# A Strassen-type matmul chain on one core: the last quad of the first up stage in another product order, its block sums a tick sooner, down slabs converted as soon as their area is open

## The chip, the cores and the metric

One Trainium2 chip, one of its cores. The metric is the device time of one execution in microseconds (us); a kernel's time is the median of three runs. Engines are named as in the profile: PE is TensorE's matmul, PEld its weight load, DVE is VectorE, ACT ScalarE, POOL GpSimd, SP SyncE, whose queue issues the DMAs.

## The reference

Attention over 4 batches, 12 heads, 448 tokens of width 64, then two dense feed-forward blocks on the 1792 x 768 result:

```
q_n, k_n = rmsnorm(q, g_q), rmsnorm(k, g_k)
attn = softmax(q_n @ k_n.T / sqrt(64)) @ v          # 4 x 12 x 448 x 64
x = attn as 1792 x 768
h = maximum(x @ w_in, 0.0);  x = (h * h) @ w_out    # first block, hidden width 2048
g = x @ w_gate                                       # second block, hidden width 1536
out = (silu(g) * (x @ w_val)) @ w_out2
```

The weights arrive in double precision, q, k and v in single; the result is wanted in single.

## The kernel before

The attention comes first and is not touched. The two blocks follow, each as an up stage and a down stage: up stage 0 (`w_in`), down stage 0 (`w_out`), up stage 1 (`w_gate`, `w_val`), down stage 1 (`w_out2`). Activations lie transposed, features on the 128 partitions and tokens along the row, 448 tokens to a slot of the tile `xacc`.

Every matrix product is done by seven products P1 to P7 on 2 x 2 blocks instead of eight (a Strassen form with the block sums T1 to T4). Each operand is split in a high part, rounded to the matmul's format, and a low part, the rest, so that a product of two 128-blocks is three matmuls: high x high, high x low, low x high. ACT makes a high part by a cast, DVE the low part by a subtraction. Weights' parts lie in a ring of five buffers (`ring`), activations' parts in units (`xab`, `xat`, `xb`, `xlast`).

*Up stage.* The loop `up` runs over quads (pairs of weight slabs, 8 in stage 0, 12 in stage 1), products and two token halves `tp`. One step is 9 matmuls of 128 x 448. A step's result is taken out of PSUM by ACT or DVE (`after`, `outer`), passed through relu and square by ACT (`finish_sum`), and becomes a block B11, B12, B21 or B22 of the hidden activations. DVE forms the sums T1 to T4 of these (`sum_of`), at the due times that `put` sets. Each block that the down stage needs is sent to DRAM (`send`, L1056, name `hid`).

*Down stage.* The loop `down` runs over 7 products x 8 groups g (6 in stage 1) in the order P2 P5 P3 P1 P6 P7 P4. One step is 18 matmuls. For step n a load brings the hidden block back (`stage`, L1269, `dn<-hid`) into one of three staging places, ACT casts its high part (`cleave(n, 0)`, L1282), DVE subtracts the low part (`cleave(n, 1)`, shown with the helper's line L1097); the parts go in one of three `hbuf` buffers. The load of step n + 3 needs the staging place that the low part of step n empties. Down weights lie in the area `dn`: half of the slabs of stage 0 were converted early and kept in DRAM, and are fetched again (`bring`, L380, `dn<-wkeep`); six slabs are converted straight into the area (`area_job`): double precision arrives as two 32-bit words, ACT writes the scaled high word (L292), DVE does one TENSOR_SCALAR (L294) and two SCALAR_TENSOR_TENSOR (L265). In the second block all slabs are kept ones, so there is no area job.

*What sets the order.* The program's order is written by Python at build time. Each engine works its instructions off in this order. After every step `pump` gives DVE a budget in us (1.2 a step in the up stage; unspent budget is carried over, up to 2.0), and takes from two streams, weights for the ring and conversions, what it pays for. Block sums (`run_sums`) and the cleaves follow behind. The list `where` says which unit holds which activation part, `hsplit` which units the `hbuf` buffers take over, and `open_down` puts the area in the place of the units 7 to 12 (`xb`) once the last product that reads them is done. In the last quad the order is P1, P4 of the quad before, P5, P6, P2, P7, P3, and P4 closes the stage; the area opens behind P7.

The gate of `area_job` before the change asks that a down step has begun:

```
yield act(lambda: None, gate=lambda: state["step"] >= 100 * ph)
```

## Time and profile before

| | |
|---|---|
| three runs | 1133.16, 1138.66, 1143.78 us, median 1138.66 |
| the profiled execution | 1143.64 us, its span 1141.8 us |
| PE busy | 1124.7 us, 99% of the span |
| DVE busy | 872.8 us, 76% |
| ACT busy | 637.0 us, 56% |
| granted TensorE clock | 1.000 |

The span runs from the first to the last instruction; the execution's own time is 1.84 us longer. Up stage 0 ends at 458.39 us and up stage 1 at 982.08 us in the span. A matmul's end in the profile is modelled, so lengths of matmul groups overlap; starts are the better measure.

### The profile page before, as it was taken

How to read it: one execution, taken by the hardware profiler on the slowest of the kernel's cores; microseconds unless marked ns; L12 is line 12 of the kernel's file. 1: busy time of each engine (PE TensorE's matmuls, PEld its weight loads, DVE VectorE, ACT ScalarE, POOL GpSimd, SP SyncE). 2: the span in 40 equal slices, each digit the busy share in tenths (PEclk: the TensorE clock that was granted, in tenths of full speed). 3: DMA queues.
4: the chain of work that ended last, by engine and by line, in shares of the span. 5: the costliest groups of instructions: out<-in, count | busy, mean ns of one | idle time of the engine just before them, and what ended most of it. 6: DMA issues, size and time to landing. Idle time of an engine off the chain costs nothing.

```text
span 1141.8 us, 17075 instructions
## 1 busy us (share of the span) xinstructions
PE 1124.7 (99%) x6164; PEld 946.3 (83%) x6164; DVE 872.8 (76%) x1253; ACT 637.0 (56%) x1047; POOL 212.2 (19%) x220
## 2 busy tenths in 40 slices
PE   8999999999999999999999999999999999999998
PEld 5555555559899999899999999999999999989998
DVE  7677888759998886998557778978787795775554
ACT  6787887656866776545544545444443434355332
POOL 5899899841000000000000000000000000000000
PEclk9999999999999999999999999999999999999999
DMA  5444322111888988966443302646464651784553
GB/s 169 122 114 126 102 92 83 47 30 30 256 297 257 305 279 269 366 211 204 157 122 121 113 1 100 227 157 208 135 210 132 211 185 53 241 287 136 179 169 138
DMA packets 116676, 189.60 MB, mean 166 GB/s; under 512 B 13936, under 2 KB 97648, under 8 KB 116592
## 3 DMA queue, kind: packets, MB, share of 16 engines
q1 hardware_dynamic: 116272, 188.52, 51.4%
q8 instruction: 48, 0.79, 0.3%
q14 instruction: 36, 0.29, 0.1%
q10 hardware_dynamic: 320, 0.00, 0.0%
HBM read 129.11 MB, written 59.20 MB: 165 GB/s over the span
## 4 chain that ended last, share of the span: by engine, by line
PE 87%; DVE 5%; DMA 3%; ACT 2%; issue 2%; SPq 1%; POOL 0%; DVEq 0%; POOLq 0%; ACTq 0%
PE ps L1135 40%; PE ps L1324 29%; PE s L789 6%; PE s L774 6%; PE s L745 2%; PE s L713 2%; PE s L810 2%; DVE xacc L1097 1%; PE s L754 1%; ACT xacc L1100 1%; DVE xacc L127 1%; DVE ring L268 1%; DMA raw<-in_k_dram 1%; DMA raw<-in_q_dram 1%; DVE xb L150 1%
## 5 line engine op out<-in xcount | busy, mean ns | idle before, releaser
L1135 PE MATMUL ps<-xb,ring 128*128 128x448 f32 x1080 | 228.7, 367 | 0.3 <-ACT xacc L1100 0.3
L1135 PEld LDWEIGHTS ps<-xb,ring 128*128 128x128 f32 x1080 | 202.7, 188 | 19.9 <-ACT xacc L1100 0.7
L1324 PE MATMUL ps<-xat,ring 128*128 128x448 f32 x1008 | 208.7, 368 | 2.7 <-DVE xat L1097 2.7
L1324 PEld LDWEIGHTS ps<-xat,ring 128*128 128x128 f32 x1008 | 189.1, 188 | 22.1 <-DVE xat L1097 3.4
L1135 PE MATMUL ps<-xat,ring 128*128 128x448 f32 x720 | 157.5, 367 | 0.0
L1324 PE MATMUL ps<-xab,ring 128*128 128x448 f32 x756 | 154.5, 366 | 1.8 <-ACT xacc L1348 1.6
L1324 PEld LDWEIGHTS ps<-xab,ring 128*128 128x128 f32 x756 | 141.6, 188 | 14.5 <-ACT xacc L1348 2.4
L1135 PEld LDWEIGHTS ps<-xat,ring 128*128 128x128 f32 x720 | 135.2, 188 | 12.8
L1100 ACT ACTIVATE xacc<-ps 128x448 f32<-128x448 f32 x148 | 79.3, 543 | 104.0 <-PE ps L1135 92.7
L1097 DVE TENSOR_TENSOR xacc<-ps,xacc 128x448 f32<-128x448 f32 x164 | 100.1, 619 | 37.5 <-PE ps L1135 23.4
L265 DVE SCALAR_TENSOR_TENSOR conv<-xacc,conv 128x768 int32<-128x768 int32 x124 | 119.7, 965 | 3.6
L1100 ACT ACTIVATE xacc<-xacc 128x448 f32<-128x448 f32 x148 | 85.0, 577 | 66.8 <-DVE xacc L1097 64.3
L1135 PE MATMUL ps<-xab,ring 128*128 128x448 f32 x540 | 117.7, 367 | 0.0
L748 DVE TENSOR_REDUCE mxz<-s 112x2 f32<-112x896 f32 x96 | 100.4, 1089 | 19.2 <-PE s L745 19.0
L1135 PEld LDWEIGHTS ps<-xab,ring 128*128 128x128 f32 x540 | 101.3, 188 | 10.3 <-issue 0.7
L1282 ACT CAST xat<-dn 128x896 fp32r<-128x896 f32 x56 | 52.9, 944 | 100.6 <-PE ps L1324 64.1
L268 DVE TENSOR_TENSOR ring<-conv,ring 128x384 fp32r<-128x384 f32 x127 | 70.7, 566 | 43.3 <-ACT ring L513 42.1
L780 POOL TENSOR_TENSOR sg<-p 112x896 f32<-112x896 f32 x46 | 96.8, 2106 | 15.0 <-ACT p L776 15.0
L776 ACT ACTIVATE p<-s 112x896 f32<-112x896 f32 x96 | 87.9, 920 | 20.7 <-PE s L774 16.3
L1097 DVE TENSOR_TENSOR xat<-dn,xat 128x896 fp32r<-128x896 f32 x56 | 60.9, 1088 | 37.8 <-ACT xat L1282 37.7
L1097 DVE TENSOR_TENSOR xacc<-xacc 128x448 f32<-128x448 f32 x148 | 88.1, 618 | 1.2
L1282 ACT CAST xab<-dn 128x896 fp32r<-128x896 f32 x42 | 39.6, 944 | 77.8 <-PE ps L1324 60.4
(97 smaller groups left out, 1361.8 us busy)
## 6 DMA issues: line engine op xcount, KB each, us to landing
hid<-xacc SPq DMA_DIRECT2D x196, 224.0 KB
dn<-hid SPq DMA_DIRECT2D x98, 448.0 KB
xacc<-in_moe_w_out_dram SPq DMA_DIRECT2D x28, 768.0 KB
xacc<-in_moe_w_in_dram SPq DMA_DIRECT2D x16, 768.0 KB
xacc<-in_moe_w_gate_dram SPq DMA_DIRECT2D x12, 768.0 KB
xacc<-in_moe_w_val_dram SPq DMA_DIRECT2D x12, 768.0 KB
wkeep<-conv SPq DMA_DIRECT2D x22, 384.0 KB
dn<-wkeep SPq DMA_DIRECT2D x44, 192.0 KB
```

Of the source, the lines that this page charges most:

```text
L265: nc.vector.scalar_tensor_tensor(out=out, in0=in0, scalar=scalar, in1=out, op0=op, op1=ALU.bitwise_or)
L268: nc.vector.tensor_tensor(out=out, in0=a, in1=b, op=ALU.subtract)
L748: nc.vector.tensor_reduce(out=mxz[:, c, 0:P:D], in_=ps[:CP, :, :S], op=ALU.max, axis=AX.X)
L774: nc.tensor.matmul(ps[:CP, a, :S], lhs, rhs, start=(w == 0), stop=(w == 3))
L776: nc.scalar.activation(out=p, in_=ps[:CP, :, :S], func=AF.Exp)
L780: nc.gpsimd.tensor_tensor(out=sg, in0=p_t[pi, 2 * w], in1=p_t[pi, 2 * w + 1], op=ALU.add)
L789: nc.tensor.matmul(ps[s, :S], v_t[pi][:, a, c * D:(c + 1) * D], p[:, a, :], start=(c == 0), stop=(c == NCH - 1),)
L1097: eng.tensor_tensor(out=o, in0=a, in1=b, op=op)
L1100: nc.scalar.activation(out=slot(s), in_=src, func=func)
L1135: nc.tensor.matmul(ps, w[:, wi, kk * P:(kk + 1) * P], xk[:, xi, kk * S:(kk + 1) * S], start=bool(first and mm == 0), stop=(mm == 3 * KT - ...
L1282: nc.scalar.copy(k[:, 0], src)
L1324: nc.tensor.matmul(ps_of(ps[tp, o]), w[:, wi, o * P:(o + 1) * P], h[:, hi, tp * S:(tp + 1) * S], start=bool(first and m == 0), stop=(g == ...
```

## The change

1. In up stage 0 the last quad runs P1, P5, P6, P3, P2, P7, P4 (P4 of the quad before still behind P1) instead of P1, P5, P6, P2, P7, P3, P4. The weight of P3 is formed in the scratch buffer `s_`, so that P2's weight block is left whole. The area opens behind P2, which is again four steps ahead of the stage's end; the loads, fetches and first cleaves that hung on P7 and P3 hang on P2 and P7 (`final`). Up stage 1 keeps its order.
2. Two activation parts change places (`where`), and the `hbuf` buffers lie in `xab` in down stage 0 and in `xat` in down stage 1 (`hsplit`), the other way round than before.
3. For the last group the sum T3 is due after 1 tick instead of 2 and T2 after 2 instead of 3, in both up stages; T1 after 1 instead of 2 in stage 0.
4. An area job may start as soon as the area is open, instead of at the first down step.

```
-        (dict(zip(names, (0, 1, 2, 3, 12, 4, 6))), dict(zip(names, (7, 8, 5, 9, 10, 11, 13)))),
-        (dict(zip(names, (0, 7, 6, 2, 8, 9, 3))), dict(zip(names, (1, 10, 13, 5, 11, 12, 4)))),
+        (dict(zip(names, (0, 1, 2, 3, 12, 4, 6))), dict(zip(names, (7, 8, 11, 9, 10, 5, 13)))),
+        (dict(zip(names, (0, 7, 6, 4, 8, 9, 1))), dict(zip(names, (3, 10, 13, 5, 11, 12, 2)))),
...
-    hsplit = (3, 0)
+    hsplit = (1, 3)
+    final = (("P2", "P7"), ("P7", "P3"))
...
-                mid.extend((p, q_) for p in ("P5", "P6", "P2", "P7", "P3"))
+                mid.extend((p, q_) for p in (
+                    ("P5", "P6", "P3", "P2", "P7") if (ph, q_) == (0, n - 1) else ("P5", "P6", "P2", "P7", "P3")))
...
     def area_job(ph, f, i):
-        yield act(lambda: None, gate=lambda: state["step"] >= 100 * ph)
+        yield act(lambda: None, gate=lambda: dn.get("ph") == ph)
...
+                    if (ph, q_) == (0, nq - 1):
+                        yield dve(0.55, minus, s_, a12, a11, gate=idle_("s"))
+                        yield from block((ph, "P3", q_), s_, "s")
+                        yield from block((ph, "P2", q_), a12, key(q_, "a12"), since=lambda: -1, done=over(q_, 0))
+                        yield from block((ph, "P7", q_), a21, key(q_, "a21"), since=lambda: -1)
+                        continue
...
-            for new, needs, wait in (("T1", ("B11", "B12"), 1 + end), ("T3", ("B22", "T1"), 2),
-                                     ("T2", ("B22", "T1"), 3), ("T4", ("B21", "T2"), 2 - end)):
+            for new, needs, wait in (("T1", ("B11", "B12"), 1 + end * ph), ("T3", ("B22", "T1"), 2 - end),
+                                     ("T2", ("B22", "T1"), 3 - end), ("T4", ("B21", "T2"), 2 - end)):
...
-            if last and (p, tp) in (("P3", 1), ("P4", 0)):
-                early = ("P3", "P4").index(p)
+            if last and (p, tp) in ((final[ph][1], 1), ("P4", 0)):
+                early = int(p == "P4")
...
-                if q_ == last and tp == 1 and p == "P7":
+                if q_ == last and tp == 1 and p == final[ph][0]:
                     open_down(ph)
...
-                if q_ == last and p == "P3":
+                if q_ == last and p == final[ph][1]:
                     bring(ph, 1 + 2 * tp)
```

Line numbers in the changed kernel are 1 to 8 higher: L1105 there is L1097 here, L1064 L1056, L1275 L1269, L266 L265, L295 L294, L269 L268, L252 L251, L382 L380.

Three places show what the change moves.

DVE at the end of up stage 0, in the kernel before, from the last result taken out of PSUM (`xacc<-ps_3373`) on. `ring1_83` is the low part of the first down weight, `xat<-dn` a low part of a hidden block, the first of them for step 0:

```order
L1097 TENSOR_TENSOR xacc_62<-ps_3373,xacc_62 128x448
L268 TENSOR_TENSOR ring1_83<-dn_5095,ring1_83 128x384
L1097 TENSOR_TENSOR xat_3139<-dn_5095,xat_3139 128x896
L268 TENSOR_TENSOR ring2_84<-dn_5095,ring2_84 128x384
L268 TENSOR_TENSOR ring3_85<-dn_5095,ring3_85 128x384
```

DVE at the same place in the changed kernel, from the last result taken out of PSUM (`xacc<-ps_3375`, product P7) on:

```order
L1105 TENSOR_TENSOR xacc_62<-ps_3375,xacc_62 128x448
L295 TENSOR_SCALAR dn_5093<-dn_5093 128x2x384
L266 SCALAR_TENSOR_TENSOR dn_5093<-xacc_62,dn_5093 128x2x384 x2
L1105 TENSOR_TENSOR xacc_62<-xacc_62 128x448
L269 TENSOR_TENSOR ring1_83<-dn_5093,ring1_83 128x384
L295 TENSOR_SCALAR dn_5093<-dn_5093 128x2x384
L266 SCALAR_TENSOR_TENSOR dn_5093<-xacc_62,dn_5093 128x2x384
L1105 TENSOR_TENSOR xacc_62<-xacc_62 128x448
L1105 TENSOR_TENSOR xab_72<-dn_5093,xab_72 128x896
```

Between the last result and the low part of step 0 there was one instruction; now there are eight: a whole conversion, half of the next, two block sums and the ring's low part.

SP's queue in down stage 0 from the load for step 5 to the load for step 7, before (`dn<-hid` is a load, `hid<-xacc` a send of a block, `xacc<-in_moe_w_out` a raw slab, `dn<-wkeep` a fetched half slab):

```order
L1269 DMA dn_5095<-hid_4764 128x896
L380 DMA dn_5095<-wkeep_4186 128x384
L380 DMA dn_5095<-wkeep_5006 128x384
L1056 DMA hid_5236<-xacc_62 128x448
L251 DMA xacc_62<-in_moe_w_out_dram 128x1536
L1269 DMA dn_5095<-hid_4989 128x896
L380 DMA dn_5095<-wkeep_4253 128x384
L1056 DMA hid_5269<-xacc_62 128x448
L1056 DMA hid_5236<-xacc_62 128x448
L251 DMA xacc_62<-in_moe_w_out_dram 128x1536
L1269 DMA dn_5095<-hid_5198 128x896
```

And the same stretch of SP's queue in the changed kernel, from the row behind the load for step 5 on:

```order
L382 DMA dn_5093<-wkeep_4186 128x384
L382 DMA dn_5093<-wkeep_5022 128x384
L1064 DMA hid_5248<-xacc_62 128x448
L1064 DMA hid_5250<-xacc_62 128x448
L1064 DMA hid_5248<-xacc_62 128x448
L252 DMA xacc_62<-in_moe_w_out_dram 128x1536
L1275 DMA dn_5093<-hid_4989 128x896
L382 DMA dn_5093<-wkeep_4253 128x384
L1064 DMA hid_5250<-xacc_62 128x448
L1064 DMA hid_5280<-xacc_62 128x448 x2
L252 DMA xacc_62<-in_moe_w_out_dram 128x1536
L1275 DMA dn_5093<-hid_5214 128x896
```

Six sends stand ahead of the load for step 7 where there were three.

SP's queue in down stage 1 from the load for step 6 to the load for step 7, before:

```order
L1269 DMA dn_8901<-hid_6989 128x896
L380 DMA dn_8901<-wkeep_7716 128x384
L380 DMA dn_8901<-wkeep_8715 128x384
L1056 DMA hid_9061<-xacc_62 128x448
L1056 DMA hid_9030<-xacc_62 128x448
L1269 DMA dn_8901<-hid_7427 128x896
```

And in the changed kernel:

```order
L1275 DMA dn_8901<-hid_6989 128x896
L382 DMA dn_8901<-wkeep_7716 128x384
L382 DMA dn_8901<-wkeep_8715 128x384
L1064 DMA hid_9062<-xacc_62 128x448
L1064 DMA hid_9064<-xacc_62 128x448
L1064 DMA hid_9032<-xacc_62 128x448
L1064 DMA hid_9062<-xacc_62 128x448
L1275 DMA dn_8901<-hid_7427 128x896
```

Two more sends stand ahead of the load for step 7.

## Rows read from the trace of the kernel before

**Rows 1.** The page: busy time by engine; the granted clock in 40 slices.

```profile
PE 1124.7 (99%) x6164; PEld 946.3 (83%) x6164; DVE 872.8 (76%) x1253; ACT 637.0 (56%) x1047; POOL 212.2 (19%) x220
...
PEclk9999999999999999999999999999999999999999
```

**Rows 2.** Timeline of PE, 456 to 500 us: start, length, idle before and releaser.

```profile
456.57 1.99 PE L1135 MATMUL ps<-xlast,ring 128*128 128x448 f32 x9
458.39 11.31 PE L1324 MATMUL ps<-xat,ring 128*128 128x448 f32 x55
471.32 3.91 PE L1324 MATMUL ps<-xat,ring 128*128 128x448 f32 x18 [1.63 <-DVE xat L1097]
476.27 24.03 PE L1324 MATMUL ps<-xat,ring 128*128 128x448 f32 x115 [1.03 <-DVE xat L1097]
```

**Rows 3.** Stretches: length, busy PE, PEld, DVE, ACT, POOL; PEclk, DMA share, GB/s.

```profile
469.60:471.30 1.70, 0.10 (x1) 0.00 (x0) 1.70 (x3) 0.25 (x1) 0.00 (x0) 1.00 1.11 398
...
476.30:480.00 3.70, 3.70 (x18) 3.38 (x19) 3.70 (x7) 2.28 (x3) 0.00 (x0) 1.00 1.01 403
```

**Rows 4.** Timeline of DVE, 453 to 476 us.

```profile
453.12 0.62 DVE L1097 TENSOR_TENSOR xacc<-ps,xacc 128x448 f32<-128x448 f32 x1 [1.20 <-PE ps L1135]
454.94 0.62 DVE L1097 TENSOR_TENSOR xacc<-ps,xacc 128x448 f32<-128x448 f32 x1 [1.20 <-PE ps L1135]
455.49 0.55 DVE L268 TENSOR_TENSOR ring<-dn,ring 128x384 fp32r<-128x384 f32 x1
456.64 1.09 DVE L1097 TENSOR_TENSOR xat<-dn,xat 128x896 fp32r<-128x896 f32 x1 [0.61 <-ACT xat L1282]
...
463.73 0.55 DVE L268 TENSOR_TENSOR ring<-dn,ring 128x384 fp32r<-128x384 f32 x1
464.20 0.55 DVE L294 TENSOR_SCALAR dn<-dn 128x768 int32<-128x768 int32 x1
464.79 1.95 DVE L265 SCALAR_TENSOR_TENSOR dn<-xacc,dn 128x768 int32<-128x768 int32 x2
466.66 1.15 DVE L1097 TENSOR_TENSOR xacc<-xacc 128x448 f32<-128x448 f32 x2
...
470.19 1.08 DVE L1097 TENSOR_TENSOR xat<-dn,xat 128x896 fp32r<-128x896 f32 x1
...
475.14 1.08 DVE L1097 TENSOR_TENSOR xat<-dn,xat 128x896 fp32r<-128x896 f32 x1
```

**Rows 5.** Timeline of ACT: the casts of the high parts for steps 0 and 7.

```profile
455.66 0.95 ACT L1282 CAST xat<-dn 128x896 fp32r<-128x896 f32 x1 [0.30 <-DMA dn<-hid]
...
482.43 0.95 ACT L1282 CAST xat<-dn 128x896 fp32r<-128x896 f32 x1 [2.51 <-DMA dn<-hid]
```

**Rows 6.** Timeline of SP's queue: the load for step 7 of down stage 0.

```profile
476.24 0.32 SPq L1269 DMA_DIRECT2D dn<-hid  x1
```

**Rows 7.** Timeline of PE in down stage 1, behind its start at 982.08 us.

```profile
982.08 22.54 PE L1324 MATMUL ps<-xab,ring 128*128 128x448 f32 x109
1004.79 1.28 PE L1324 MATMUL ps<-xab,ring 128*128 128x448 f32 x5 [0.17 <-DVE xab L1097]
1007.38 1.49 PE L1324 MATMUL ps<-xab,ring 128*128 128x448 f32 x6 [1.31 <-ACT xacc L1348]
1009.18 41.01 PE L1324 MATMUL ps<-xab,ring 128*128 128x448 f32 x201 [0.32 <-ACT xacc L1348]
```

**Rows 8.** Timeline of ACT at the same place.

```profile
1005.96 0.94 ACT L1282 CAST xab<-dn 128x896 fp32r<-128x896 f32 x1 [1.93 <-DMA dn<-hid]
1006.80 0.96 ACT L1348 COPY xacc<-ps 128x448 f32<-128x448 f32 x2
1008.60 1.98 ACT L1348 COPY xacc<-ps 128x448 f32<-128x448 f32 x4 [0.83 <-DMA hid<-xacc]
```

**Rows 9.** Timeline of SP's queue at the same place: sends, and the load for step 7.

```profile
998.67 0.95 SPq L1056 DMA_DIRECT2D hid<-xacc  x2
999.71 0.44 SPq L1269 DMA_DIRECT2D dn<-hid  x1
```

More of the change, by code (lines that the diff above doesn't have):

```diff
@@ L1237, in up @@
                 if q_ == last and tp == 1:
-                    level = {"P1": 0, "P6": 1, "P2": 2, "P3": 3, "P7": 4, "P4": 5}.get(p)
-                    if level is not None:
-                        state["down"] = 100 * ph + level
+                    state["down"] = ph
                 if ph == 0 and q_ >= 3 and not state["third"] and len(free) >= 8 and all(s in free for s in (3, 4, 5, 6)):
                     claim_third()
-                if q_ == last and tp == 1 and p == "P7":
+                if q_ == last and tp == 1 and p == final[ph][0]:
                     open_down(ph)
```

## The prediction, made before the changed kernel was run

> **What bounds the kernel now.** I read the busy table first: PE is busy 1124.7 of 1141.8 us, so at most 17 us of the span are gaps, and the granted clock is full in all 40 slices [rows 1]. A change that leaves the matmuls alone can only move these gaps. Next came PE's own timeline at the two places that the change touches, the passages from an up stage to its down stage. In the first, PE runs from 458.39 us through 55 matmuls, which is 3 steps of 18 and the first matmul of step 3, then waits for DVE's low part (1.63 us), does 18 more and waits for the next low part (1.03 us); from 476.27 us on it runs without a gap past 500 us [rows 2]. In that first gap DVE is busy 1.70 of 1.70 us [rows 3]: it is not waiting but late. Its timeline says with what: low parts start at 470.19 and 475.14 us, behind a TENSOR_SCALAR and pairs of SCALAR_TENSOR_TENSOR, the conversions of the down slabs, and behind block sums [rows 4]. Before the stage's end the same engine idles 1.20 us ahead of each result, since it follows PE in lockstep [rows 4]. In the second passage the gaps are 0.17, 1.31 and 0.32 us [rows 7]; the two longer ones end with copies on ACT that free PSUM banks, and these stand behind a cast that waited 1.93 us for its load [rows 8].
>
> Measured by starts: nine matmuls take 458.39 - 456.57 = 1.82 us, 0.202 each [rows 2]; I use 0.203 in the down stage. Step 3's second matmul was due at 458.39 + 55 x 0.203 = 469.56 and started at 471.32: 1.76 us lost. Then 471.32 + 18 x 0.203 = 474.97 against 476.27: 1.30 us. Together 3.06 us in the first passage; the profile's idle figures, 2.66 us, are smaller since the ends of matmuls are modelled.
>
> **The change part by part.** *Nothing for the product order itself.* P3 now comes first of the three and needs a weight formed by one more subtraction before it; all of this is made several us ahead of use, where DVE idles between results, and the step count behind the open area (four) is the same. Swapped units and the `hbuf` move change names, not instructions. I cost these at 0; the cover is DVE's idle time before each result, 1.20 us in a step of 1.82 [rows 4], against about 0.5 us for a subtraction. If it were gone, the same 0.5 us would be the price.
>
> *The conversion ahead of step 0's low part.* This is the main term. The order places eight instructions between the last result taken from PSUM and the low part of step 0, where there was one. The builder pays them from budget saved up earlier, but that saved time is gone: DVE takes the last result when PE has finished it, at 454.94 us, and PE does not move. From there, by start-to-start distances in [rows 4]: result to next 0.55 (454.94 to 455.49); TENSOR_SCALAR 0.59 (464.20 to 464.79); a pair of SCALAR_TENSOR_TENSOR 1.87 (464.79 to 466.66), so 0.94 for one; a ring low part 0.47 (463.73 to 464.20); a block sum 0.55, taken from the result's distance. So the low part of step 0 starts at 455.49 + 0.59 + 1.87 + 0.55 + 0.47 + 0.59 + 0.94 + 0.55 = 461.05 and ends 1.08 later, at 462.13 us; before it started at 456.64 and ended at 457.73 [rows 4], 0.66 us ahead of PE. Nothing holds it besides this: its high part is cast at 455.66 [rows 5], and may come 1 us later behind the conversion's ACT part. PE's first matmul needs only the high parts and starts at 458.39; the second needs the low part and is due at 458.59. It waits until 462.13: 3.54 us lost.
>
> *The stalls that go.* Counted on from 461.05 in the changed order, the work ahead of step 3's low part is: low part of step 0, two ring parts, two sums, low part 1, a ring part, one SCALAR_TENSOR_TENSOR, low part 2, a ring part, TENSOR_SCALAR, one SCALAR_TENSOR_TENSOR, three sums, one more SCALAR_TENSOR_TENSOR, low part 3. With 1.08 for a low part that is 12.36 us, so it ends at 473.4; with 1.00 from the start of a low part to the next instruction (464.20 - 463.73 being 0.08 under that row's length too) it is 473.2. It is due when PE has issued 54 more matmuls: 462.13 + 54 x 0.203 = 473.09. So 0 to 0.3 us are lost, I take 0.2. Step 4's low part follows 1.55 us later, near 474.9, and is due near 477: no loss. The 3.06 us of before vanish. What is late next is step 7: see below. Net of the first passage so far: +3.54 + 0.2 - 3.06 = +0.7 us.
>
> *The queue of SP in down stage 0.* The sums come a tick sooner and their sends with them. From load 5 to load 7 the queue holds six sends where it held three. A send costs SP 0.475 us (0.95 for two) [rows 9], so 1.4 us for three, and their 3 x 224 KB take 1.7 us at the 403 GB/s of that stretch [rows 3]. Load 7 went out at 476.24 [rows 6] and its cast was done at 482.43 + 0.95 = 483.38 [rows 5]; a low part of 1.08 makes 484.5, against a due time of 476.27 + 54 x 0.203 = 487.23: 2.8 us to spare. In the changed kernel it is due 0.7 later and comes up to 3.1 later: the reserve shrinks to 0.4. The copies that free the PSUM banks for step 8 stand behind that cast in ACT's queue, as in the second passage. The price lies between 0 and 1.7 us (the data time of the three sends); I take 0.5, nearer to 0, since the reserve holds by the sum.
>
> *The queue in down stage 1.* Two more sends stand ahead of load 7: 0.95 us [rows 9]. This load is the one that the cast at 1005.96 waits for, and behind the cast stand the copies that PE waits 1.31 us for [rows 7, 8]. So that gap grows by up to 0.95. Against that, the later copies waited 0.83 us for a send to finish [rows 8], which now starts sooner, and PE's 0.32 us may go. Bounds: +0.95, and -1.8 if all three gaps (0.17 + 1.31 + 0.32) went; value +0.5, since the queue is read from the order and the relief is only likely.
>
> Sum: 0.7 + 0.5 + 0.5 = +1.7 us. On the profiled execution's 1143.64 us that is 1145.3; that execution lies 5 us above the median of the three runs, so the forecast of the median is 1138.66 + 1.7 = 1140.4 us. A difference of 1% is 11.4 us, about what a measurement of this kernel tells from no change; the three runs alone span 10.6 us. So this counts as no change.
>
> **The rivals.** *A: the stalls go and none comes.* For it: the conversions are the stalls' cause, and they do start about 8 us sooner (464.20 against 455.49 [rows 4]). Against it: DVE is strictly in order, and step 0's low part stands behind 5.5 us of work with 3.1 us until PE needs it. It would take the ops to overlap, or the second passage to profit from its sooner sums in full. Then -3.06 and up to -1.8: 1138.66 - 3.1 - 0.9 = 1134.7 us.
>
> *B: the clock falls in the new gap, and the kernel is slower.* The gap at step 0 is 3.5 us in one piece. The gaps that this trace shows there are 1.63 and 1.03 us, and the granted clock was 1.00 in and behind them [rows 2, 3]. If a gap twice as long took TensorE from 2.4 to 1.2 GHz, each step of 18 matmuls would take 7.3 instead of 3.65 us until it rose again. Two steps cost +7.3: 1140.4 + 7.3 = 1147.7 us. From three steps on (+11) it is slower by 1%. What decides is whether PE stands still longer than in any of these rows. The Trainium skill (TensorE: Matmul & The Clock Gate, "Part 1: The HAM clock gate") says that the clock gate lets half of the pulses through after PE has been idle for a while. No gap of 3.5 us is in these rows, so the trace doesn't settle it.
>
> *C: the converted slabs are not there yet.* The first raw slab is read about 8 us sooner. If it had not landed, ACT would stand at the conversion's first instruction with the relu, the ring casts and step 0's high part behind it. Each us of that adds to the 3.54. Against it: in the kernel before, the first conversion on DVE followed the instruction ahead of it without a wait [rows 4], so the slab lay there already; for how long the rows don't say. With 3 us: 1143.4 us.
>
> **How the numbers follow.** Forecast (+0.5 to +3.5): 0.65. A: 0.18. B: 0.09. C: 0.08. The likeliest case, 1140.4, has its own range of 1139 to 1142. The bounds reach from 1138.66 - 3.06 - 1.8 = 1133.8 to 1138.66 + 3.54 + 0.3 + 1.7 + 0.95 - 3.06 = 1142.1 without B, and to 1149 with it. As three runs of the same kernel lie 5 us to either side of their median, the range is 1133.5 to 1147.5. Faster by over 1% needs more than every gap of both passages, 0.02; slower by over 1% needs B for three steps, 0.04; within 1%: 0.94.
>
> **What would show it.** Right: on DVE, TENSOR_SCALAR right behind the last result, near 455.5 us, and the first `xab<-dn` near 461; on PE, one matmul at the start of down stage 0, then a gap of about 3.5 us that ends with a low part, and no gap at steps 3 and 4 worth over 0.3 us. In down stage 1 the gap that the copies end is 1.5 to 2.3 us. Wrong: no gap at step 0 (then A); a granted clock below 1.00 behind it (B); ACT idle ahead of the first conversion with a DMA as releaser (C); a gap of over 2 us near step 7 or 8 (the queue term is too small).

## The result, and the profile after

Twenty executions of each kernel: before 1135.69 us median (1133.16 to 1144.39), after 1145.70 (1136.69 to 1153.47); ratio of the times 1.0067, 95% interval 1.0044 to 1.0091, so +7.6 us (5 to 10). The ratio is taken over all the executions and is not that of the two medians, which lie 10.0 us apart. A second comparison (twelve against twenty-three, told below) gave 1.0048, 1.0017 to 1.0080, or +5.5 us. Ratios leave out executions over 1.5% above the fastest of their kernel, three in the whole study. The change costs some 6 us. The forecast was +1.7.

The page of after has the same picture as [rows 1]: PE bounds, and the granted clock reads 9 in every slice, which is too coarse for what follows.

```profile
PE 1114.9 (98%) x6164; PEld 947.6 (83%) x6164; DVE 872.2 (77%) x1253; ACT 636.4 (56%) x1047; POOL 212.7 (19%) x220
...
PEclk9999999999999999999999999999999999999999
```

After's timeline of PE in the first passage, against [rows 2]: start, length, idle before and releaser.

```profile
458.68 0.37 PE L1330 MATMUL ps<-xab,ring 128*128 128x448 f32 x1
462.36 27.16 PE L1330 MATMUL ps<-xab,ring 128*128 128x448 f32 x125 [3.32 <-DVE xab L1105]
489.88 0.47 PE L1330 MATMUL ps<-xab,ring 128*128 128x448 f32 x1 [0.36 <-ACT xab L1288]
491.01 3.93 PE L1330 MATMUL ps<-xab,ring 128*128 128x448 f32 x18 [0.66 <-DVE xab L1105]
495.40 9.79 PE L1330 MATMUL ps<-xab,ring 128*128 128x448 f32 x47 [0.46 <-DVE xab L1105]
```

One matmul, a wait, then a row of 125 with no idle time in it. The gaps at steps 3 and 4 are gone; three new ones stand at steps 7 and 8. The row of 125 hides something: 124 starts at 0.2026 us would take 25.1 us, and it runs 27.16 less the last matmul's 0.37, 26.8. The windows behind the gap (length, then busy time of PE, PEld, DVE, ACT, POOL, PEclk, DMA share, GB/s) say why:

```profile
462.00:464.00 2.00, 1.64 (x5) 1.47 (x6) 2.00 (x5) 2.00 (x5) 0.00 (x0) 0.63 0.93 280
464.00:466.00 2.00, 2.00 (x7) 1.78 (x6) 2.00 (x4) 0.69 (x1) 0.00 (x0) 0.52 0.76 291
466.00:468.00 2.00, 2.00 (x11) 1.85 (x11) 2.00 (x3) 0.33 (x1) 0.00 (x0) 1.00 0.81 249
```

In the 4 us behind the gap the granted clock is 0.63 and 0.52 (0.50 would be the lower of its two levels, 1.2 GHz, throughout), and PE does 7 matmuls in 2 us where it does 11 afterwards. Length and idle columns do not show this; only starts or the clock do. The Trainium skill (TensorE: Matmul & The Clock Gate, "Part 1: The HAM clock gate") says that half of the pulses go through after an idle spell; the level of the rows agrees.

After's DVE at the same place, against [rows 4]:

```profile
455.23 0.62 DVE L1105 TENSOR_TENSOR xacc<-ps,xacc 128x448 f32<-128x448 f32 x1 [0.66 <-PE ps L1143]
455.77 0.55 DVE L295 TENSOR_SCALAR dn<-dn 128x768 int32<-128x768 int32 x1
456.35 1.95 DVE L266 SCALAR_TENSOR_TENSOR dn<-xacc,dn 128x768 int32<-128x768 int32 x2
...
461.23 1.08 DVE L1105 TENSOR_TENSOR xab<-dn,xab 128x896 fp32r<-128x896 f32 x1
```

Step 0's low part ends at 462.31. At steps 7 and 8 the releasers are ACT's cast and the low part behind it, and the cast waits for its load. ACT's cast for step 7, against [rows 5], and the load for step 7 in SP's queue, against [rows 6]:

```profile
488.89 0.94 ACT L1288 CAST xab<-dn 128x896 fp32r<-128x896 f32 x1 [3.05 <-DMA dn<-hid]
```

```profile
477.60 1.56 SPq L1064 DMA_DIRECT2D hid<-xacc  x3
479.26 0.65 SPq L252 DMA_DIRECT2D xacc<-in_moe_w_out_dram  x1
480.32 0.82 SPq L1275 DMA_DIRECT2D dn<-hid  x1
```

The load goes out 4.1 us later than before (480.32 against 476.24) and takes 8.6 us until its cast starts, where it took 6.2: both the queue and the data are late. In the kernel before this load went out as soon as its staging place was free (step 4's low part ended at 475.14 + 1.08 = 476.22 [rows 4]). In after that low part ended at 474.55, and the load stood in the queue for another 5.8 us: the three sends ahead of it took 1.56, and 1.3 us passed at a fetch (`dn<-wkeep`, 477.10) that waited for an earlier load. What PE waits for at step 7 is the low part behind the cast. In before it stood on DVE behind a conversion:

```profile
484.81 1.08 DVE L1097 TENSOR_TENSOR xat<-dn,xat 128x896 fp32r<-128x896 f32 x1
```

It ended at 485.89, 27.5 us into the stage; in after at 490.95, 32.3 us into it. Down stage 1, against [rows 7, 8]:

```profile
976.84 23.55 PE L1330 MATMUL ps<-xat,ring 128*128 128x448 f32 x114
1003.40 16.89 PE L1330 MATMUL ps<-xat,ring 128*128 128x448 f32 x82 [3.01 <-ACT xacc L1354]
```

One gap of 3.01 in the place of 0.17, 1.31 and 0.32.

Here "by starts" means the time at which a matmul starts, less what the matmuls ahead of it take back to back. Step 8's second matmul is the 146th of the stage; 495.40 - 458.68 - 145 x 0.2026 = 7.3 us lost, against 3.06 before: +4.3. In down stage 1, 1003.40 - 976.84 - 114 x 0.203 = 3.4 against 1009.18 - 982.08 - 120 x 0.203 = 2.7: +0.7. Together +5.0 in this pair of executions. (The second pair, told below, does not show the +0.7.)

Yet after's profiled span is 1137.3 us and before's 1141.8. The two executions ran at different paces with the same granted clock, 1.00, over long stretches. One row of each, 720 to 780 us, from the groups by line (count, busy, mean ns):

```profile
L1135 PE MATMUL ps<-xb,ring 128*128 128x448 f32 x108 | 22.6, 368 | 0.0
```

```profile
L1143 PE MATMUL ps<-xb,ring 128*128 128x448 f32 x109 | 22.6, 365 | 0.0
```

368 ns is before, 365 after; per matmul the starts are 0.2067 and 0.2026 us apart. Over before's 506 us from 476 to 982 us, all at the lower pace, these 2% are 10.0 us, more than the change is worth. So spans of single executions are not compared below; the measure is the count of matmuls in the first 42 us of each down stage, where the waits lie. Before did 191 and 195 there, after 173 and 192. The pace is in this measure too: 42 us at the lower one hold 4 matmuls fewer.

### The profile page after: what moved, and what is told of

Read it like the earlier page. It is cut to its first block, busy times and chain, and to the rows that moved or that the text cites. A ratio compares the mean times of both kernels' runs of the same rounds, so it can differ in the third digit from the quotient of the medians.

```text
span 1137.3 us, 17069 instructions
## 1 busy us (share of the span) xinstructions
PE 1114.9 (98%) x6164; PEld 947.6 (83%) x6164; DVE 872.2 (77%) x1253; ACT 636.4 (56%) x1047; POOL 212.7 (19%) x220
## 4 chain that ended last, share of the span: by engine, by line
PE 83%; DMA 5%; DVE 5%; ACT 2%; issue 2%; SPq 1%; POOL 0%; DVEq 0%; ACTq 0%; POOLq 0%
PE ps L1143 39%; PE ps L1330 27%; PE s L797 6%; PE s L782 6%; PE s L753 2%; PE s L721 2%; DMA dn<-hid 2%; PE s L818 2%; DMA hid<-xacc 1%; DVE xacc L1105 1%; DMA dn<-wkeep 1%; DMA raw<-in_q_dram 1%; DVE ring L269 1%; PE s L762 1%; DVE xb L151 1%
## 5 line engine op out<-in xcount | busy, mean ns | idle before, releaser
L1143 PE MATMUL ps<-xb,ring 128*128 128x448 f32 x1080 | 225.5, 365 | 1.4 <-ACT xacc L1108 1.4
L1330 PE MATMUL ps<-xab,ring 128*128 128x448 f32 x1008 | 207.1, 368 | 4.8 <-DVE xab L1105 4.4
L1330 PEld LDWEIGHTS ps<-xab,ring 128*128 128x128 f32 x1008 | 190.4, 189 | 21.3 <-DVE xab L1105 5.5
L1330 PE MATMUL ps<-xat,ring 128*128 128x448 f32 x756 | 153.9, 366 | 3.0 <-ACT xacc L1354 3.0
L1330 PEld LDWEIGHTS ps<-xat,ring 128*128 128x128 f32 x756 | 141.9, 188 | 14.9 <-ACT xacc L1354 3.4
L1143 PE MATMUL ps<-xat,ring 128*128 128x448 f32 x720 | 154.1, 365 | 0.0
L1143 PEld LDWEIGHTS ps<-xat,ring 128*128 128x128 f32 x720 | 135.3, 188 | 10.6
L1105 DVE TENSOR_TENSOR xacc<-ps,xacc 128x448 f32<-128x448 f32 x164 | 100.0, 620 | 34.0 <-PE ps L1143 20.4
L266 DVE SCALAR_TENSOR_TENSOR conv<-xacc,conv 128x768 int32<-128x768 int32 x124 | 120.4, 971 | 3.7
L1143 PE MATMUL ps<-xab,ring 128*128 128x448 f32 x540 | 116.4, 366 | 0.0
L1288 ACT CAST xab<-dn 128x896 fp32r<-128x896 f32 x56 | 52.8, 944 | 102.7 <-PE ps L1330 66.3
L1143 PEld LDWEIGHTS ps<-xab,ring 128*128 128x128 f32 x540 | 101.4, 188 | 8.6 <-issue 0.7
L269 DVE TENSOR_TENSOR ring<-conv,ring 128x384 fp32r<-128x384 f32 x126 | 70.2, 567 | 39.1 <-ACT ring L521 38.9
L1105 DVE TENSOR_TENSOR xab<-dn,xab 128x896 fp32r<-128x896 f32 x56 | 61.0, 1089 | 41.2 <-ACT xab L1288 41.0
L1105 DVE TENSOR_TENSOR xacc<-xacc 128x448 f32<-128x448 f32 x148 | 88.4, 619 | 1.8 <-DMA hid<-xacc 0.7
L1288 ACT CAST xat<-dn 128x896 fp32r<-128x896 f32 x42 | 39.6, 944 | 80.5 <-PE ps L1330 60.0
```

The source lines that it names most:

```text
L266: nc.vector.scalar_tensor_tensor(out=out, in0=in0, scalar=scalar, in1=out, op0=op, op1=ALU.bitwise_or)
L269: nc.vector.tensor_tensor(out=out, in0=a, in1=b, op=ALU.subtract)
L1105: eng.tensor_tensor(out=o, in0=a, in1=b, op=op)
L1143: nc.tensor.matmul(ps, w[:, wi, kk * P:(kk + 1) * P], xk[:, xi, kk * S:(kk + 1) * S], start=bool(first and mm == 0), stop=(mm == 3 * KT - ...
L1288: nc.scalar.copy(k[:, 0], src)
L1330: nc.tensor.matmul(ps_of(ps[tp, o]), w[:, wi, o * P:(o + 1) * P], h[:, hi, tp * S:(tp + 1) * S], start=bool(first and m == 0), stop=(g == ...
```

## The experiments

Twelve runs, in three groups; the last two are the two kernels once more. Each group shared the runs of the kernel before on its chip. All profiles are of one execution each.

**The late gate back** in the changed kernel.

```
-        yield act(lambda: None, gate=lambda: dn.get("ph") == ph)
+        yield act(lambda: None, gate=lambda: state["step"] >= 100 * ph)
```

> The changed kernel with the area job's gate of before (a down step must have begun); order, units and sums stay changed. Theory 1 (the conversions ahead of step 0's low part cost 3.5 us, and the clock falls in that gap): no gap over 0.5 us in step 0 of down stage 0, granted clock 1.00 from 458 to 470 us, and one or two gaps of together 2 to 3 us come back at steps 3 and 4; the gap in down stage 1 stays near 3 us. Time 0 to +3 us against the kernel before, some 5 us under the changed kernel. Theory 2 (product order, sums and SP's queue cost it, not the conversions): +6 to +9 us against the kernel before, as the changed kernel.

Measured: 1141.71 us, ratio 1.0008 (0.9978 to 1.0039). PE:

```profile
459.31 11.31 PE L1330 MATMUL ps<-xab,ring 128*128 128x448 f32 x55
472.39 20.38 PE L1330 MATMUL ps<-xab,ring 128*128 128x448 f32 x90 [1.77 <-DVE xab L1105]
493.18 7.08 PE L1330 MATMUL ps<-xab,ring 128*128 128x448 f32 x33 [0.41 <-DVE xab L1105]
```

The gap at step 0 is gone and the one at step 3 is back, so in the changed kernel the gate alone decides where DVE is late. The clock fell behind the 1.77 us too (0.79 and 0.87 in the next two windows of 5 us). 186 matmuls in 42 us: without the gate 2.6 us of the loss are gone. The time follows: the interval lies below that of after's first comparison, though it overlaps that of the second. In down stage 1, where the gate has no job to act on, this execution has one gap of 2.02 us instead of the 3 expected, and 197 matmuls; so much do executions differ there.

**The gate alone** in the kernel before (the same edit the other way round).

> The kernel before with the new gate alone; order, units and sums stay as before. Theory 1: PE waits in step 0 of down stage 0 as well, 2 to 3.5 us, for a low part or for a PSUM bank whose last result DVE takes late, and the gaps at steps 3 and 4 shrink under 0.5 us each. If the clock stays at 1.00, -1 to +1 us against the kernel before; if it falls behind the gap, +2 to +5 us. Theory 2: no gap over 1 us in step 0, -1 to +1 us.

Measured: 1135.78 us, ratio 0.9963 (0.9934 to 0.9992).

```profile
462.42 0.37 PE L1324 MATMUL ps<-xat,ring 128*128 128x448 f32 x1
464.96 35.33 PE L1324 MATMUL ps<-xat,ring 128*128 128x448 f32 x173 [2.17 <-DVE xat L1097]
```

With the old order and sums the gate gives one gap of 2.17 us, a clock of 1.00 behind it and nothing at steps 3, 4, 7 and 8: 197 matmuls, 1 us better than before. The time is 4.2 us better by the ratio, more than either theory allowed. The gate hurts only together with the rest of the change, where two block sums more stand ahead of that low part on DVE (2 x 0.54 of the 1.15 us between this gap and after's 3.32; the gap is 3.32 with the old due times as well, see below, so these two come with the order).

**Filling the gap**: sixteen extra matmuls at the head of step 0 of the changed kernel, into the bank that the first real one starts anew.

```
+                        if ph == 0 and n == 0 and tp == 0 and o == 0:
+                            for _ in range(16):
+                                nc.tensor.matmul(ps_of(ps[0, 0]), w[:, 0, :P], h[:, 0, :S], start=True, stop=True,
+                                                 skip_group_check=True)
```

> The changed kernel with 16 more matmuls of 128x448 at the head of step 0 of down stage 0, on operands that are ready, into a bank that the step's first matmul overwrites; they fill 3.2 us of the 3.5 us gap and add nothing to the result. Theory 1: the first low part ends where it did (near 462.3 us), PE has no gap over 0.6 us there, the granted clock stays 1.00 from 458 to 470 us, and the time falls by what the slow clock took, 1.7 us in the profiled run and up to 5 us in others: +2 to +6 us against the kernel before. Theory 3 (the clock falls there for another reason than PE standing still): it falls all the same, and the time is that of the changed kernel, +6 to +9 us.

Measured: 1143.57 us, ratio 1.0039 (1.0003 to 1.0075), which overlaps after's interval. PE:

```profile
461.25 22.82 PE L1334 MATMUL ps<-xab,ring 128*128 128x448 f32 x108
484.56 0.47 PE L1334 MATMUL ps<-xab,ring 128*128 128x448 f32 x1 [0.50 <-ACT xab L1288]
485.69 3.77 PE L1334 MATMUL ps<-xab,ring 128*128 128x448 f32 x17 [0.65 <-DVE xab L1105]
489.74 0.47 PE L1334 MATMUL ps<-xab,ring 128*128 128x448 f32 x1 [0.28 <-ACT xab L1288]
490.87 3.98 PE L1334 MATMUL ps<-xab,ring 128*128 128x448 f32 x18 [0.66 <-DVE xab L1105]
```

The clock stayed at 1.00 in this passage and nothing was won there: step 6 now waits as well, and step 7's second matmul starts 490.87 - 458.00 = 32.9 us into the stage, in after 491.01 - 458.68 = 32.3. PE was early at a door that the loads open. That the time did not fall has a second possible reason: in down stage 1 this execution had gaps of 0.83, 0.51 and 2.59 us with the clock at 0.66 behind them, 175 matmuls where after did 192. Whether that goes with the filling is open.

**The old due times of the sums** in the changed kernel.

```
-            for new, needs, wait in (("T1", ("B11", "B12"), 1 + end * ph), ("T3", ("B22", "T1"), 2 - end),
-                                     ("T2", ("B22", "T1"), 3 - end), ("T4", ("B21", "T2"), 2 - end)):
+            for new, needs, wait in (("T1", ("B11", "B12"), 1 + end), ("T3", ("B22", "T1"), 2),
+                                     ("T2", ("B22", "T1"), 3), ("T4", ("B21", "T2"), 2 - end)):
```

> The changed kernel with the due times of the sums T1, T2, T3 of before. Theory 1: the gap at step 0 of down stage 0 stays at 3 to 3.7 us with a granted clock under 1.00 behind it; the gaps at steps 7 and 8 (1.5 us together in the profile of the changed kernel) shrink to 0 to 1 us since fewer sends stand ahead of load 7, and the gap in down stage 1 shrinks from 3.0 to between 1.5 and 2.5 us in all: 1 to 3 us under the changed kernel, +4 to +7 us against the kernel before. Theory 2: the loss sits here: +0 to +2 us.

Measured: 1146.98 us, ratio 1.0044 (1.0002 to 1.0086). PE, and a window behind the gap:

```profile
457.15 0.37 PE L1330 MATMUL ps<-xab,ring 128*128 128x448 f32 x1
460.84 44.51 PE L1330 MATMUL ps<-xab,ring 128*128 128x448 f32 x206 [3.32 <-DVE xab L1105]
```

```profile
460.00:465.00 5.00, 4.16 (x11) 3.73 (x12) 5.00 (x8) 3.11 (x6) 0.00 (x0) 0.50 0.93 303
```

No gap at steps 7 and 8. The same gap at step 0 cost more clock here (0.50 in this window, 0.87 in the next five us), so only 179 matmuls. This lateness of PE is a part of why no gap shows: step 7's low part ended 30.6 us into the stage, against 32.3 in after and 27.5 in before, and PE came to it at 31.8. So the old due times win back 1.7 of the 4.8 us. In down stage 1 the gap at the copies is back to 1.29, but others of 0.86 and 0.33 came with it: the 121st matmul starts 27.6 us into the stage, in after 27.9.

**The low part first**: in the changed kernel, the cleaves of the last steps written ahead of `pump` and `run_sums`.

```
-            pump(rate)
-            run_sums()
             if last and (p, tp) in ((final[ph][1], 1), ("P4", 0)):
...
+            pump(rate)
+            run_sums()
```

> The changed kernel with the high and low parts of the last two up steps written ahead of that step's conversions and sums, so that step 0's low part stands in front of the conversions on DVE. Theory (DVE is in order and its work in these steps is fixed, so the wait only changes place; what is saved is the clock): the gap of 3.3 us at step 0 breaks into pieces of 0.9 to 1.5 us at steps 0, 1 and perhaps 3, with a sum of 3 to 4 us, granted clock 1.00 behind them; gaps of 0.4 to 0.7 us at steps 7 and 8 stay. Against the changed kernel the clock's share comes back, 2 to 3 us: ratio to the kernel before 1.003 to 1.005. Rival 1 (only the position of that one low part matters): no gap over 0.5 us at steps 0 to 3, ratio 1.000 to 1.002. Rival 2 (neither gap nor clock counts, the time is lost elsewhere): ratio 1.006 to 1.008.

Measured: 1142.80 us, ratio 1.0036 (1.0007 to 1.0065). PE:

```profile
462.20 3.98 PE L1330 MATMUL ps<-xab,ring 128*128 128x448 f32 x18 [1.32 <-DVE xab L1105]
467.21 7.57 PE L1330 MATMUL ps<-xab,ring 128*128 128x448 f32 x36 [1.03 <-DVE xab L1105]
474.96 11.58 PE L1330 MATMUL ps<-xab,ring 128*128 128x448 f32 x54 [0.18 <-DVE xab L1105]
487.20 3.71 PE L1330 MATMUL ps<-xab,ring 128*128 128x448 f32 x17 [0.66 <-DVE xab L1105]
491.88 0.47 PE L1330 MATMUL ps<-xab,ring 128*128 128x448 f32 x1 [0.97 <-ACT xab L1288]
493.01 12.16 PE L1330 MATMUL ps<-xab,ring 128*128 128x448 f32 x51 [0.66 <-DVE xab L1105]
```

The gap broke into the pieces that the theory named and the clock held behind them until the waits at steps 6 and 7 (0.90 and 0.76 in the windows of 5 us from 490 us on), and again step 7's second matmul came 493.01 - 460.51 = 32.5 us into the stage (it began at 460.51). The ratio is the theory's, but not its reason: in this execution the clock's share was spent in waits for the loads, and the clock fell there after all: 168 matmuls.

**The order alone**: the late gate and the old sums together in the changed kernel (the edits of the first and fourth experiment).

> The changed kernel with the late gate of before and the due times of before for the sums: the product order and the units that go with it are all that is left. Theory (the order itself costs nothing): no gap at step 0, one gap of 1.8 to 2.7 us at step 3, none at steps 7 and 8, the gap in down stage 1 that ends with copies 1.2 to 1.5 us; ratio to the kernel before 0.998 to 1.001. Rival (the order is what costs): gaps at step 0 or later that are not in the kernel before, ratio 1.003 or more.

Measured: 1137.71 us, ratio 0.9982 (0.9951 to 1.0013). PE, then the sends of SP's queue between the loads for steps 5 and 7, and the load for step 7:

```profile
474.11 31.10 PE L1330 MATMUL ps<-xab,ring 128*128 128x448 f32 x139 [2.96 <-DVE xab L1105]
```

```profile
470.01 0.90 SPq L1064 DMA_DIRECT2D hid<-xacc  x2
...
474.93 2.46 SPq L1064 DMA_DIRECT2D hid<-xacc  x4
...
478.68 0.77 SPq L1275 DMA_DIRECT2D dn<-hid  x1
```

One gap at step 3, of 2.96 us, more than expected, with the clock at 0.51 in the five us behind it; none at steps 7 and 8; 1.42 in down stage 1. The order by itself costs nothing that the comparison tells. But the six sends are here with the due times of before, so they come with the order and its units and not with the sooner sums; and the profile has 180 matmuls in the first passage, 11 or 2.2 us fewer than before.

**The gate with the low part first**, on the kernel before (the edits of the second and fifth experiment).

> The kernel before with the new gate alone, as in an earlier run of this study (ratio 0.9963), and the low part of step 0 written ahead of the last conversions. Theory: the one gap of 2.17 us at step 0 falls to 0.9 to 1.0 at step 0 and 0.3 to 0.5 at step 1, no gap at steps 3, 4, 7 and 8, clock 1.00: 1 us less than the gate alone, ratio 0.993 to 0.997, the fastest so far. Rival (the wait only changes place, here too): gaps with a sum of 2 us or more, ratio 0.996 to 0.998.

Measured: 1135.78 us, ratio 0.9969 (0.9937 to 1.0001). PE:

```profile
462.00 3.90 PE L1324 MATMUL ps<-xat,ring 128*128 128x448 f32 x18 [0.79 <-DVE xat L1097]
466.18 14.87 PE L1324 MATMUL ps<-xat,ring 128*128 128x448 f32 x72 [0.27 <-DVE xat L1097]
481.93 23.37 PE L1324 MATMUL ps<-xat,ring 128*128 128x448 f32 x114 [0.89 <-DVE xat L1097]
```

The gap shrank as expected and another of 0.89 came at step 5: 196 and 196 matmuls, the best pair, but no better in time than the gate alone. Of the two, only the gate alone is faster than the kernel before by more than its interval (up to 0.9992; here up to 1.0001).

**Filling, with the old sums** (third and fourth experiment together).

> The changed kernel with both remedies of the earlier runs: sixteen matmuls that fill the gap at step 0 (they write a bank that the real first matmul starts anew) and the sums' due times of before. Theory (the clock behind the gap and the loads held up by the sends are separate costs, so the savings add): fill saved 3.2 us, the old sums 2.6, the changed kernel is at 7.6, so 1.8 us stay: ratio 1.000 to 1.003; clock 1.00 in the first 10 us of the stage, no gaps at steps 7 and 8, the gap in down stage 1 that ends with copies 1.2 to 1.5 us. Rival (both remedies mend the same cost): ratio 1.0035 to 1.005.

Measured: 1147.46 us, ratio 1.0047 (1.0008 to 1.0086): the savings do not add in the time. In the passage they do better than either: 182 matmuls after the sixteen extra ones, step 7's second matmul at 30.4 us instead of 32.9. But gaps of 0.65 and 0.48 us stay there, and in down stage 1 two of 1.73 and 1.62 us came with a clock of 0.70, 174 matmuls. The old sums leave no gap at step 7 only while a low clock makes PE late as well.

What these experiments and the two repeats below show of step 7 of down stage 0, read from SP's queue, DVE and PE. "Place free" is the end of step 4's low part, which empties the staging place of load 7:

| kernel | sends between loads 5 and 7 | load 7 goes out after place free, us | step 7's low part ends, us into the stage | matmuls in 42 us, both down stages |
|---|---|---|---|---|
| before; again | 3; 3 | 0.0; 0.0 | 27.5; 27.4 | 191, 195; 193, 190 |
| gate alone | 3 | 0.0 | 27.1 | 197, 191 |
| gate, low part first | 3 | 0.0 | 27.4 | 196, 196 |
| order alone | 6 | 1.3 | 28.6 | 180, 194 |
| late gate (order and sums) | 6 | 1.9 | 29.4 | 186, 197 |
| old sums (order and gate) | 6 | 4.4 | 30.6 | 179, 193 |
| filled, old sums | 6 | 5.2 | 30.4 | 182, 174 |
| after; again | 6; 6 | 5.8; 5.0 | 32.3; 32.1 | 173, 192; 174, 184 |
| filled | 6 | 5.9 | 32.8 | 170, 175 |
| low part first | 6 | 5.5 | 32.4 | 168, 191 |

The early gate alone does not hold the load up, the order alone does by 1.3 us. Order and gate together make 3.0 of the 4.8 us by which step 7's low part is late in after, the sooner sums the rest.

**Breaks in PE's run**: the kernel before with ten waits in up stage 1, where it has none (`pad` is a small tile that the kernel already had).

```
+            if ph and p == "P1" and tp == 0 and q_ >= 2:
+                for _ in range(1):
+                    nc.tensor.matmul(ps, w[:, 0, :P], xk[:, 0, :S], start=True, stop=True, skip_group_check=True)
+                    nc.vector.tensor_copy(pad, ps[:, :8])
```

> The kernel before with ten short breaks in the second up stage, one per quad: an extra matmul into the bank that the next product starts anew, and a copy of eight of its columns on DVE that the product's first matmul has to wait for. It asks what sets PE's pace: at a granted clock of 1.00 throughout, the profiles so far show two levels in the up stages, 0.2016 us (248 to 249 matmuls in 50 us) and 0.205 us (243 to 244), and the level changes nowhere but at the passages where PE waits. Theory (the level is drawn anew at each wait of PE and kept until the next): with ten waits of 0.5 to 3 us the stretches of 126 matmuls between them show both levels, changing from one to the next at some of the breaks; a row of a stretch at the slow level is 0.4 to 0.5 us longer. Rival 1 (the level belongs to an execution or to a stage): all stretches of the stage at one level. Rival 2 (it drifts with time or temperature): values between the two. Span 1140 to 1165.

Measured: one execution, span 1182.8, longer than expected. Of the stretches behind the breaks, two in full (54 matmuls and the nine behind them show the pace):

```profile
843.47 5.47 PE L1139 MATMUL ps<-xab,ring 128*128 128x448 f32 x18 [3.21 <-DVE pad L1135]
848.77 3.81 PE L1139 MATMUL ps<-xat,ring 128*128 128x448 f32 x18
...
856.08 11.10 PE L1139 MATMUL ps<-xb,ring 128*128 128x448 f32 x54
867.01 1.99 PE L1139 MATMUL ps<-xat,ring 128*128 128x448 f32 x9
...
872.42 3.98 PE L1139 MATMUL ps<-xab,ring 128*128 128x448 f32 x18 [1.39 <-DVE pad L1135]
876.24 3.88 PE L1139 MATMUL ps<-xat,ring 128*128 128x448 f32 x18
...
883.68 11.32 PE L1139 MATMUL ps<-xb,ring 128*128 128x448 f32 x54
894.84 2.02 PE L1139 MATMUL ps<-xat,ring 128*128 128x448 f32 x9
```

54 matmuls take 10.93 us from start to start in the first stretch (867.01 - 856.08) and 11.16 in the next. Of the ten stretches five run at either level, none between, and within the stage the level changes only at a break. That bears the theory out for these stretches. The same rows price the clock: behind the six breaks of 3.05 to 3.54 us the first 18 matmuls took 5.26 to 6.57 us (here 848.77 - 843.47 = 5.30), behind the four of 1.32 to 1.39 us 3.75 to 3.82.

**Long breaks**: `range(4)` in the same place.

> The same with each break four times as long: four extra matmuls, each waiting for the copy of the one before. Theory (a wait draws the level anew, whatever its length): both levels as with the short breaks, waits of 3 to 6 us in sum, and the granted clock below 1.00 behind some of them, as behind the 3.3 us gap of the changed kernel, so that a stretch of 126 matmuls can be some us longer. Rival (only short waits do it): one level in all stretches where the clock is 1.00. Span 1165 to 1210.

Measured: one execution, span 1211.9. Again both levels, 0.2067 in three of the ten stretches behind breaks, 0.2026 in seven. The waits of one break sum to 2.1 to 4.8 us, the granted clock of the whole execution is 0.976 (0.988 with the short breaks). So both levels occur behind either length.

**The changed kernel again, and the kernel before against itself.**

> The changed kernel as it is, a second time, for a second profile and twelve more times. Theory (direct price of the waits 5 to 6 us, the rest the level that PE's pace happens to take in the stretches): ratio to the kernel before 1.003 to 1.009; on PE again one matmul, a gap of 3.2 to 3.5 us with the clock below 1.00 behind it, gaps at steps 7 and 8 of 0.4 to 1.0 us, a gap of 2.5 to 3.2 us in down stage 1; the level of the pace (248 or 244 matmuls in 50 us) need not be the same in each stretch as in the first profile. Rival (the levels belong to the kernel): the same level in each of the three stretches as in its first profile, 248 to 249 in all.

> The kernel before as it is, against itself: what the comparison tells from no change, and a second profile. Both theories: ratio 1.000 within 0.003; gaps of 1.5 to 1.8 and 0.9 to 1.4 us at steps 3 and 4. Theory (the pace's level is drawn at the waits): the stretch from 520 to 970 us need not run at 243 to 244 matmuls in 50 us again. Rival (the level belongs to the kernel): 243 to 244 there and 248 before 450 us, as in the first profile.

Measured: after 1144.28 us, ratio 1.0048 (1.0017 to 1.0080); before 1135.55, ratio 0.9984 (0.9950 to 1.0018). In after the gap at step 0 is 3.33, with clocks of 0.67 and 0.65 in two windows of 5 us; only the 0.48 us at step 8 is left of the late gaps, 2.85 us in down stage 1 with 0.72 behind it: 174 and 184 matmuls. Here more clock was lost and fewer waits, with the same count as in the first profile (173). In before the gaps at steps 3 and 4 are 1.30 (1.5 to 1.8 expected) and 1.03, 193 and 190 matmuls. Its down stage 1, from the first row and from the 121st matmul on:

```profile
984.77 19.05 PE L1324 MATMUL ps<-xab,ring 128*128 128x448 f32 x91
...
1012.96 12.23 PE L1324 MATMUL ps<-xab,ring 128*128 128x448 f32 x59 [0.34 <-ACT xacc L1348]
```

The 121st matmul starts 28.2 us into the stage here, 27.1 in before's first profile, 27.9 and 27.7 in the two of after, all four mostly at the higher pace. So the waits up to there do not tell the two kernels apart. The level differs from the first profile in up stage 0 (74 or 75 matmuls in 15 us where there were 76) and is again the lower one from 520 to 970 us; in after it differs in down stage 1. And the long breaks' program, which is that of before up to its first break at 722 us, ran from 520 us to there at the higher pace (248 or 249 matmuls in 50 us, in before 243 or 244). So the level does not belong to the kernel.

## Why the prediction was right or wrong

- *No change by its own bound of 1%*, and the measured +7.6 us is below it: right. The size was not: +1.7 against 5 to 10, and 1145.70 us lies above the 1139 to 1142 given for the forecast, though inside the whole range, which allowed 5 us to either side for scatter. B's number, 1147.7, was the nearer one, but not by B's way: the clock gave 1.7 of its 7.3 us.
- *Nothing for the product order itself*: no time that the comparison tells (0.9951 to 1.0013), but a part of the mechanism was missed. I looked for the cover in DVE's idle time; what the order and its units moved is SP's queue, six sends where there were three and four or five ahead of load 5 where there were two.
- *The conversion ahead of step 0's low part*: right. Low part 461.05 to 462.13 predicted, 461.23 to 462.31 measured; 3.54 us lost predicted, 462.36 - 458.68 - 0.20 = 3.48 measured. The late gate put back removes it.
- *The stalls that go*: right. 3.06 us gone; at step 3 0.2 us was allowed, and no idle time shows.
- *The queue of SP in down stage 0*: this term failed. I took 0.5 of 0 to 1.7, "since the reserve holds by the sum". The reserve was read too large. In before, step 7's low part did not follow its cast, done at 483.38, but came from 484.81 to 485.89 (its row stands with the result above). Against the due time of 487.23 that leaves 1.3 us to spare and not 2.8. The lateness was taken too small. By the sum the cast came up to 3.1 us later; it came 6.5 later (488.89 against 482.43), 4.1 until the load's issue and 2.4 from issue to cast. I put the sends down to the sooner sums; they come with the order. And I counted only from load 5 on. Behind the early conversions the low parts of steps 0 and 1 end late, and loads 3 and 4 wait for the staging places that these empty: they go out 4.3 and 3.3 us later into the stage than before, and load 5, behind five sends instead of two, at 12.2 us instead of 6.7. In after's profile it cost 0.53 + 0.93 + 0.74 = 2.2 us by starts at steps 7 and 8. The list of wrong signs named one gap of over 2 us near there; it came in three pieces. The old sums took 1.7 us off the lateness, not all of it.
- *The clock*, rival B, held at 0.09, did happen, in both profiles of after. In the first it cost 26.8 - 25.1 = 1.7 us, a quarter of the 7.3 I had priced. It does not simply add: two kernels that kept the clock at step 0 (filled, low part first) and one execution that lost more of it (after's second profile, step 8's second matmul at 495.17 - 458.66 = 36.5 us against 36.7) came to step 7 or 8 no sooner and no later than after's first, since the late loads bind there. So the two failed steps are one number of 2.2 + 1.7 us, and with 3.48 - 3.06 they give the +4.3.
- *Down stage 1*: +0.5 predicted, gap of 1.5 to 2.3; measured 3.01 and 2.85, too small by about 0.7. As for the cost, the +0.7 by starts of the first pair is not shown to be the change's: before's second profile came to its 121st matmul later than either of after's, and with the old sums that matmul starts only 0.3 us sooner. What did come in after's second profile is a clock of 0.72 behind the gap (184 matmuls against 190). The sums join three gaps into one; that this costs time is open.
- *A* (stalls go and none comes) and *C* (slabs not there): no sign of either; DVE's first conversion follows the result without a wait.
- What stays open is the difference between the +4.3 of the first passage, which both profiles of after bear out, and the ratios' +5.5 and +7.6. The levels of PE's pace are large enough to make it (10.0 us over one stretch), but how often each kernel meets which level was not measured. The gate alone, with and without the low part first, had one of 24 executions above 1141 us, the kernel before 24 of 70 on the same two chips. That suggests that most of the 4 us (by the ratios) by which these two are ahead lies there and only 1 us in fewer waits; it isn't shown.

## What to carry to other kernels

Read a transfer's reserve from the instruction that PE waits for (here the low part, 1.3 us), not from the cast ahead of it (2.8). When sends move, count them ahead of the earlier loads of the same ring too, price the queue and the data both, and look for what makes the earlier loads go out late. When two resources are late at the same step, curing the earlier lateness (here the gap, or the clock behind it) buys nothing until the later door opens; count work done since the stage's start rather than idle time. Before two single profiles are compared, compare the pace of the same steady matmuls in both.

## What was not expected of the hardware

- PE's steady pace has two levels at a granted clock of 1.00, 0.2026 and 0.2067 us per matmul of 128 x 448. It may change where PE waits: with ten added waits it was 0.2067 behind five of them, with ten longer ones behind three. It can change without a wait that the rows show, too: in before the last 18 matmuls of up stage 1 take 3.72 us from start to start (978.36 to 982.08), the first 18 of down stage 1, which follow at once, 3.65. In the rows the mean length of a matmul is 365 or 368 ns. One long stretch at the lower pace is 10.0 us, as much as the three times of before spread. What picks the level was not found.
- The granted clock does not follow from the length of a gap alone: 1.00 behind gaps of 2.17 us and, in down stage 1 of after, 3.01 us; 0.79 behind 1.77, 0.51 behind 2.96, and below 1.00 behind all six of the short breaks of over 3 us, by the time of their first 18 matmuls (0.53 to 0.68 in three that were read).
